# A third buffer for turned q and four moves of work around it in the last pass of a fused SSM and SwiGLU gradient kernel

## The chip, the cores and the metric

The kernel runs on one core of one Trainium2 chip. The metric is the device time of one execution in microseconds (us). A core has five engines with instruction queues of their own: TensorE (PE, matmul; its weight loads are listed as PEld), VectorE (DVE), ScalarE (ACT), GpSimd (POOL) and SyncE (SP), which here only issues DMAs.

## The reference

A forward pass and its gradient with respect to the 14 inputs, for a sequence of L = 2048 rows with D = 576 channels, N = 128 states for each channel and F = 4608 hidden columns, inputs in bfloat16:

```
x  = A_u
xn = layernorm(x)                                 # over D
K  = real(sum_n C * exp(dt * A * l) * (dt * B))   # D x L kernel of the state space model
s  = causal_conv(xn, K) + xn * Dskip
h  = silu(xn @ w1) * (xn @ w3)
g  = silu(h @ w2)
out = x + s * g
grads = vjp(out)(grad_out)                        # for every input
```

## The kernel before, in words

The forward pass and most of the backward pass come first. The change is in the **last pass**, `phase6_inputs`, from about 1326 us to the end. It makes the gradient of x. The 2048 rows are 16 tiles of 128 rows. For each tile, 72 products are added up in PSUM (`px`): 36 blocks of the gate's gradient GG against w1 and 36 blocks of the up gradient GU against w3. A product n is two matmuls of 128x288 (L2036; the first two tiles, and the last one, go by other loops, L2072 and L2053). The tile `acts` on the left is loaded from DRAM by transposing DMAs on SP's queue (`load_acts`, L1833), GG and GU apart, two tiles ahead, into the buffer that this tile leaves: GG of tile i + 2 is asked for in the middle of tile i, GU at its end.

When a tile's products are done, `ln_bwd_tile` takes it back through the layernorm: VectorE adds the rows `gxs` to `px` (gx, L2105), ScalarE and VectorE form two means (L2155, L2158), GpSimd scales them (sc, L2163 and L2164), ScalarE makes `gxs` from them (L2165), GpSimd adds the rows `go` (L2166). The **last sum** of a tile, which makes its rows of out_1, is apart in `ln_finish`: one VectorE instruction (go, L2171), then a store on ScalarE's queue; for tiles 10 to 13 also two turned stores on GpSimd's queue (L2177). It is called after product n = 8 of the next tile. The rows gxs and go are loaded by SP (L2020, L2021) in `begin`.

Two other pieces of work are put between the products.

- **Steps** (`param_step`, `param_half`). The gradients of the model's parameters need, for each of 36 groups of channels (ch) in two halves, 8 small matmuls (et_ps, L1523) of a turned q (`qT`) against `gz`, then two products on VectorE (pr_q, L1528), each followed by a sum into `S_all` (L1531). The loads of a group (`param_loads`) are asked for two groups ahead, qT by SP, gz (L1508) and pz (L1511) by GpSimd; there are two buffers for qT. The tuple `stops` names the products behind which a step stands: (42, 66) in tile 2, (30, 60) in tile 3, (20, 50) in tiles 4, 6 and 9, none in 0, 1 and 15, and (14, 38, 62) in the others.
- **Blocks** (`phase5_blocks`), a generator that `phase5_step` moves on by one `yield` at each step. Each of five blocks of parameter rows loads `X_b` (L1589, GpSimd), takes ST from the finished sums S_all (L1594, L1595) and products of X_b (L1601 to L1603); then, one yield later, TensorE turns ST (four transposes, L1608, the **turn** of a block) and ScalarE copies it back (L1610); then VectorE makes four outputs (L1614 to L1616), which GpSimd stores (L1620), and so on up to L1637. After the last block, TensorE turns one small tile (L1641).

The steps' and the blocks' PSUM tiles come from one pool (`ps_T`) and one tile more (`ps_X`). Every queue runs in the order in which the program issues. `issue_after` binds an instruction's place behind another one in that order.

Of the kernel before, what the change touches and what calls it, by code (L numbers as in the profile page):

```python
# [14 lines left out]
BF16 = mybir.dt.bfloat16  # L15
I32 = mybir.dt.int32
I16 = mybir.dt.int16
P = 128
# [82 lines left out]
class K:  # L101
# [1231 lines left out]
    def params_open(self, S_all, ps):  # L1333
        cfg = self.cfg
        self.sums = ExitStack()
        gkp = self.sums.enter_context(self.pool(name="g_k", bufs=1, side="right"))
        self.qp = self.sums.enter_context(self.pool(name="g_q", bufs=2, side="right"))
        self.zp = self.sums.enter_context(self.pool(name="g_z", bufs=3, side="right"))
        self.prp = self.sums.enter_context(self.pool(name="g_pr", bufs=1, side="right"))
        self.S_all, self.ps_T = S_all, ps  # L1340
        self.gz = []
        for i in range(3):
            z = gkp.tile([P, 2, 2, 2, 8, cfg.LT], BF16, name=f"gz{i}")
            self.nc.vector.memset(z[:], 0.0)
            self.gz.append(z)
        self.half = 0
        self.apart = False
        self.ps_X = None
        self.loaded = {}

    def param_step(self):
        nch = self.cfg.D // 16
        if self.half == 2 * nch:
            return
        ch, dg = divmod(self.half, 2)
        with self.tc.issue_after(self.pe_last.ins):
            self.param_half(ch, dg, *self.loaded[ch])
        if dg == 1 and ch + 2 < nch:
            if self.hold is None:
                self.loaded[ch + 2] = self.param_loads(ch + 2)  # L1360
            else:
                self.hold.append(ch + 2)
        self.half += 1
# [12 lines left out]
    def conv_bwd_quarter(self, g, kp, zp, ps, T0, TQ):  # L1376
# [102 lines left out]
        for j in range(NB - 1, -1, -1):  # L1479
# [18 lines left out]
            nc.scalar.dma_start(out=self.GXN_dram[:, j * KT:(j + 1) * KT, cs], in_=gx[:])  # L1498

    def param_loads(self, ch):  # L1500
        nc, cfg = self.nc, self.cfg
        g, cc = divmod(ch, cfg.D // 64)
        gK = self.gz[ch % 3]
        qT = self.qp.tile([P, 16, cfg.N], BF16, name="qT")
        self.nat_transpose(qT[:], self.Q_dram[ch])
        put, q = (self.gp, nc.gpsimd) if self.apart else (self.sp, nc.sync)
# [8 lines left out]
    def param_half(self, ch, dg, gK, qT, pz):  # L1515
        nc, AV = self.nc, self.cfg.AV
# [8 lines left out]
        for x in range(2):  # L1525
# [4 lines left out]
                                    in1=pz[:, dg * 2 + x][:, :, None, :].to_broadcast([P, 2, 4, 4 * AV]), op=ALU.mult)  # L1530
            nc.vector.tensor_reduce(out=self.S_all[:].rearrange("p r (h c) -> p r h c", h=2)[:, :, :, d0:d0 + 2],  # L1531
                                    in_=pr[:].rearrange("p r k (h j a) -> p (r k) h j a", h=2, j=2), op=ALU.add, axis=AX.X)
# [40 lines left out]
    def phase5_blocks(self):  # L1573
# [6 lines left out]
        for j, c0 in enumerate(range(0, H, 64)):  # L1580
# [22 lines left out]
            tt(out=W[v, 1], in0=Q[v, 0, 1], in1=Q[v, 1, 0], op=ALU.add)  # L1603
            yield 0
            pt = self.ps_T.tile([P, 4, N], FP32, name="et_ps")
            with self.tc.issue_after(self.pe_last.ins):
# [40 lines left out]
    def backward(self, T0, TG, TQ, TC, TX, gctx, mats):  # L1647
# [11 lines left out]
        with ExitStack() as out:  # L1659
            wp = out.enter_context(pool(name="e_w", bufs=2))  # L1660
            self.rowp = rowp = out.enter_context(pool(name="e_w2r", bufs=1))
# [18 lines left out]
            self.hn = {}  # L1680
            self.w2Ts = {}
            self.ggs = {}
            self.tail = None
# [117 lines left out]
            wT[:-3] = sorted(wT[:-3], key=lambda part: part[0])  # L1801
            ffn.close()
            self.phase6_inputs(T2, TX, wT, acts, pool)
            self.sums.close()
# [40 lines left out]
    def phase6_load_w2(self, gi, wp):  # L1845
        nfl = self.FG // P
        w2T = wp.tile([P, nfl, self.cfg.DT, P], BF16, name="w2T")
        for fl in range(nfl):
            with self.tc.issue_after(self.hc_loads[13].ins) if gi == 0 else nullcontext():
                self.nat_transpose(w2T[:, fl], self.w2rows[gi % 2][:, fl])  # L1850
# [156 lines left out]
    def phase6_inputs(self, T2, TX, wT, acts, pool):  # L2007
# [7 lines left out]
        with pool(name="l_sb", bufs=2) as sb, pool(name="l_s1", bufs=1) as s1, \  # L2015
# [16 lines left out]
            def product(i, px, n0, n1, stops):  # L2032
                for n in range(n0, n1):
                    ai, fi, w = (sides if i else steps)[n]
                    for pi_, (po, pw) in enumerate(pieces):
                        self.pe_last = nc.tensor.matmul(px[pi_][:, 0:pw], lhsT=acts[i][:, ai, fi, :], rhs=w[:, po:po + pw],  # L2036
                                                        start=(n == 0), stop=(n == len(steps) - 1))
                    if n == 8 and i > 1:
                        self.ln_finish()
                    if n == cfg.FT - 1 and 1 < i < LT - 2:  # L2040
                        self.load_acts(i + 2, (0,), acts[i])
                    if n in stops:
                        self.param_step()
                        self.phase5_step(self.half // 2)

            n1, n2, n3 = self.ready, self.ready + 14, len(steps)
# [39 lines left out]
            acts.append(self.load_acts(3, (0,), acts[1]))  # L2086
            self.param_flush()
            blocks(1, late, True)
            self.load_acts(3, (1,), acts[1])
            for i in range(LT):  # L2090
                self.at(T2 + TX * i)
                t = self.order[i]
                px, gxs, go_t, o1, _ = opened[i] if i < 2 else begin(i)
                if i == 1:
# [9 lines left out]
                for pi_, (po, pw) in enumerate(pieces):  # L2104
                    nc.vector.tensor_tensor(out=gx[:, po:po + pw].rearrange("p (g d) -> p g d", g=4),  # L2105
                                            in0=px[pi_][:, 0:pw].rearrange("p (g d) -> p g d", g=4),
                                            in1=self.perm(gxs[:])[:, :, pi_, :], op=ALU.add)
                self.ln_bwd_tile(sm, gx, gxs, i, t, go_t, o1)
                if 1 < i < LT - 2:
                    acts.append(self.load_acts(i + 2, (1,), acts[i]))  # L2110
# [169 lines left out]
```

## Time and profile before

| | |
|---|---|
| runs | 1678.49, 1654.67, 1642.81 us; median 1654.67 |
| profiled execution | 1651.06 us, span 1648.9 us |
| TensorE | busy 1575.2 us (96% of the span) |
| VectorE | busy 1385.5 us (84%) |
| ScalarE | busy 838.3 us (51%) |
| GpSimd | busy 517.4 us (31%) |
| granted TensorE clock, mean over the span | 0.989 |
| last pass | about 1326 to 1649 us |

A time is read as follows: a run is one execution, and the profile is of another one of the same program. Busy time of an engine counts its instructions without the waits between them. In the rows of the profile, `[5.79 <-DVE ST L1594]` behind an instruction says that its engine was idle for 5.79 us before it and that VectorE's instruction of line 1594 ended the wait.

### The profile page before, as it was taken

The page shows a single profiled execution, that of the slowest core. Times are in us where ns is not written, and L with a number is a line of the kernel's source. Part 1 is how long each engine was busy: PE and PEld are TensorE (multiplying, and loading weights), DVE is VectorE, ACT ScalarE, POOL GpSimd, SP SyncE. Part 2 cuts the span into 40 slices and gives each one's busy share as a digit, 9 for nine tenths or more (in the row PEclk, how much of TensorE's full clock was granted, in tenths as well). Part 3 has the DMA queues.
Part 4 walks back from the last instruction along what each step waited for, and adds up shares of the span by engine and source line. Part 5 has one row for each costly group of instructions (what it writes and reads, how often), then busy time and mean ns, then how long its engine had stood idle before and what let it go on. Part 6 is the DMA issues. An engine that isn't in the chain of part 4 may idle for free. (4 is left out here: it accounts for less than half of the span.)

```text
span 1648.9 us, 34389 instructions
## 1 busy us (share of the span) xinstructions
PE 1575.2 (96%) x13331; PEld 1150.1 (70%) x13331; DVE 1385.5 (84%) x2145; ACT 838.3 (51%) x1520; POOL 517.4 (31%) x862
## 2 busy tenths in 40 slices
PE   6899999999999998999999999999999999989988
PEld 2554444444457776888888888888888787868866
DVE  8889998799965655998978999699989945788788
ACT  6989998766642115556555565555555301011011
POOL 7746766532242110111111111112212343325241
PEclk9999999999999999999999999999999999999999
DMA  7999999987999996576695756899999999999992
GB/s 239 347 335 360 373 344 376 380 264 249 316 294 218 240 224 207 157 213 194 191 258 161 214 185 184 234 228 253 257 244 258 243 252 232 249 211 214 210 236 64
DMA packets 616156, 408.26 MB, mean 248 GB/s; under 512 B 424698, under 2 KB 558426, under 8 KB 611386
## 3 DMA queue, kind: packets, MB, share of 16 engines
q1 hardware_dynamic: 561232, 277.45, 67.1%
q0 software_dynamic: 36576, 116.69, 21.8%
q10 hardware_dynamic: 18186, 11.95, 2.5%
q8 instruction: 104, 1.70, 0.4%
q14 instruction: 58, 0.48, 0.1%
HBM read 128.52 MB, written 188.76 MB: 192 GB/s over the span
## 5 line engine op out<-in xcount | busy, mean ns | idle before, releaser
L1982 PEld LDWEIGHTS <-xn_bf 128*128 128x128 bf16 x2304 | 224.4, 98 | 34.4 <-issue 8.2
L2036 PEld LDWEIGHTS <-acts 128*128 128x128 bf16 x1974 | 193.2, 99 | 49.3 <-issue 0.2
L1967 POOL DMA_DIRECT2D out_dram<-gw x72 | 47.3, 657 | 532.5 <-ACT gw L1984 313.4
L1528 DVE TENSOR_TENSOR pr_q<-et_ps,pz 128x1024 f32<-128x1024 f32 x144 | 175.9, 1221 | 27.5 <-PE et_ps L1523 20.1
L1123 PEld LDWEIGHTS <-xnT 128*128 128x128 bf16 x1152 | 107.8, 98 | 127.8 <-issue 20.2
L1531 DVE TENSOR_REDUCE S_all<-pr_q 128x32 f32<-128x1024 f32 x144 | 175.2, 1217 | 3.2
L1916 PE MATMUL ph<-w2T,goT 128*128 128x256 bf16 x1440 | 169.7, 273 | 1.4 <-ACT gh L1919 1.4
L1123 PE MATMUL pg<-wmB_w,xnT 128*128 128x512 bf16 x576 | 156.8, 381 | 1.3 <-DVE g_t L1142 1.0
L1957 PE MATMUL pgw<-go_o,h_n 128*128 128x288 bf16 x1152 | 153.9, 288 | 1.0 <-ACT gw L1963 1.0
L1916 PEld LDWEIGHTS <-goT 128*128 128x128 bf16 x1440 | 139.1, 98 | 18.7 <-issue 2.9
L1123 PE MATMUL pu<-wmB_w,xnT 128*128 128x512 bf16 x576 | 149.7, 379 | 0.0
L2036 PE MATMUL px<-wT,acts 128*128 128x288 bf16 x1134 | 147.3, 288 | 0.0
L1982 PE MATMUL pgw<-gu_n,xn_bf 128*128 128x256 bf16 x1152 | 133.0, 272 | 3.6 <-ACT gw L1963 3.1
L1957 PEld LDWEIGHTS <-h_n 128*128 128x128 bf16 x1152 | 112.7, 98 | 29.2 <-issue 2.1
L1982 PE MATMUL pgw<-gg_n,xn_bf 128*128 128x256 bf16 x1152 | 130.3, 273 | 0.4 <-ACT gw L1984 0.4
L1919 ACT CAST gh<-ph 128x512 bf16<-128x512 f32 x144 | 80.5, 589 | 85.1 <-PE ph L1916 78.6
L1138 ACT ACTIVATE s_t<-pg 128x512 bf16<-128x512 f32 x144 | 88.3, 613 | 55.9 <-PE pu L1132 43.9
L2155 ACT ACTIVATE go<-gx 128x576 bf16<-128x576 f32 x15 | 10.2, 683 | 185.1 <-DVE gx L2105 158.0
L813 POOL COPY KT<-k_s 64x128 bf16<-64x128 bf16 x144 | 85.1, 591 | 53.7 <-ACT k_s L810 49.0
L2036 PE MATMUL px<-wA,acts 128*128 128x288 bf16 x728 | 97.3, 290 | 0.0
L1143 ACT CAST u_t<-pu 128x512 bf16<-128x512 f32 x144 | 87.3, 606 | 6.3 <-PE pu L1123 6.2
L1152 POOL DMA_DIRECT2D G_dram<-g_t x72 | 51.5, 716 | 120.0 <-ACT g_t L1140 93.8
(338 smaller groups left out, 3244.5 us busy)
## 6 DMA issues: line engine op xcount, KB each, us to landing
U_dram<-u_t POOLq DMA_DIRECT2D x72, 256.0 KB, 6.1
H_dram<-h_t SPq DMA_DIRECT2D x72, 256.0 KB
G_dram<-g_t POOLq DMA_DIRECT2D x72, 256.0 KB, 5.7
Q_dram<-q_k SPq DMA_DIRECT2D x36, 512.0 KB
GG_dram<-gg_n SPq DMA_DIRECT2D x36, 512.0 KB
GU_dram<-gu_n SPq DMA_DIRECT2D x36, 512.0 KB
gg_n<-G_dram POOLq DMA_DIRECT2D x14, 1024.0 KB, 6.5
E_dram<-E_k SPq DMA_DIRECT2D x54, 256.0 KB
```

The lines of the kernel that those rows point to most:

```text
L813: nc.gpsimd.tensor_copy(out=KT[64 * hf:64 * hf + 64, :, ch // 9, h, d1:d1 + 8], in_=ks[64 * h:64 * h + 64, :, h, hf].rearrange("p d a -> p ...
L1123: ins = nc.tensor.matmul(pt[:], lhsT=xnT[:, c, ts], rhs=wm[w][:, c, :], start=(q == 0 and c == 0), stop=(q == 1 and c == nfull - 1))
L1138: nc.scalar.activation(out=s_t[:, :, q, :], in_=pgv, func=ACT.Silu)
L1143: self.gate_last = nc.scalar.copy(out=u_t[:, :, q, :], in_=puv)
L1152: self.u_stores[step] = nc.gpsimd.dma_start(out=dst[fb * ng:(fb + 1) * ng, :, i0:i0 + NT, :].rearrange("g p t f -> p g (t f)"), in_=src[:] ...
L1528: nc.vector.tensor_tensor(out=pr[:].rearrange("p r k e -> p r (k e)"), in0=T[x][:].rearrange("p z k h j a -> p (z k h j a)")[:, None].to_b ...
L1531: nc.vector.tensor_reduce(out=self.S_all[:].rearrange("p r (h c) -> p r h c", h=2)[:, :, :, d0:d0 + 2], in_=pr[:].rearrange("p r k (h j a) ...
L1916: self.pe_last = nc.tensor.matmul(ph[j][:, k, :].rearrange("p (a f) -> p a f", f=P), lhsT=lw, rhs=rh, start=(n == 0), stop=(n == nfull))
L1919: self.sc(lambda: nc.scalar.copy(out=gh[:, j], in_=ph[j][:]))
L1957: self.pe_last = nc.tensor.matmul(pgw[pi_][:, 0:pw], lhsT=hn[:, tt, fl * P:(fl + 1) * P], rhs=go_o[:, tt, po:po + pw], start=(tt == 0), st ...
L1982: self.pe_last = nc.tensor.matmul(pw_[:, 0:FG], lhsT=self.xn_bf[:, tt, c * P:(c + 1) * P], rhs=nat[:, tt, :], start=(tt == 0), stop=(tt == ...
L2036: self.pe_last = nc.tensor.matmul(px[pi_][:, 0:pw], lhsT=acts[i][:, ai, fi, :], rhs=w[:, po:po + pw], start=(n == 0), stop=(n == len(steps ...
```

## The change

Four edits, all in the last pass:

1. **Third buffer for the turned q.** The pool `e_w`, which before had two buffers of w2T, now has one double tile of w2T and is free in the last pass. One of every three qT is placed there, and each qT is asked for three groups ahead instead of two (`param_q`, `qTs`, `third`). gz and pz stay two groups ahead.
2. **Last sum later.** `ln_finish` is called at the next tile's first step, if that is at product 20 or before, and bound behind that step's last sum in S_all; else after product 8, as before.
3. **Turn later.** A second `yield 0` ahead of a block's turn, in all blocks but the last.
4. **Rows ahead of GU.** `begin(i + 1)` is called at the end of tile i ahead of GU's load, instead of at the start of tile i + 1.

```diff
 def param_step(self):
...
         if dg == 1 and ch + 2 < nch:
             if self.hold is None:
                 self.loaded[ch + 2] = self.param_loads(ch + 2)
+                if self.third and ch + 3 < nch:
+                    self.third[1] = self.third[1] or ch
+                    self.qTs[ch + 3] = self.param_q(ch + 3, None if (ch - self.third[1]) % 3 else self.third[0])
...
+    def param_q(self, ch, third=None):
+        if third is None:
+            qT = self.qp.tile([P, 16, self.cfg.N], BF16, name="qT")
+        else:
+            qT = third.tile([P, 16, self.cfg.N], BF16, name="qT", tag="w2T")
+        self.nat_transpose(qT[:], self.Q_dram[ch])
+        return qT
+
     def param_loads(self, ch):
...
-        qT = self.qp.tile([P, 16, cfg.N], BF16, name="qT")
-        self.nat_transpose(qT[:], self.Q_dram[ch])
+        qT = self.qTs.pop(ch, None)
+        if qT is None:
+            qT = self.param_q(ch)
...
 def param_half(self, ch, dg, gK, qT, pz):
...
-            nc.vector.tensor_reduce(out=self.S_all[:].rearrange("p r (h c) -> p r h c", h=2)[:, :, :, d0:d0 + 2],
+            self.pr_last = nc.vector.tensor_reduce(out=self.S_all[:].rearrange("p r (h c) -> p r h c", h=2)[:, :, :, d0:d0 + 2],
...
 def phase5_blocks
...
             yield 0
+            if c0 + R < H:
+                yield 0
             pt = self.ps_T.tile([P, 4, N], FP32, name="et_ps")
...
 # the w2 loads of an earlier phase
-            wp = out.enter_context(pool(name="e_w", bufs=2))
+            wp = out.enter_context(pool(name="e_w", bufs=1))
...
-        w2T = wp.tile([P, nfl, self.cfg.DT, P], BF16, name="w2T")
+        if self.w2TT is None:
+            self.w2TT = wp.tile([P, 2, nfl, self.cfg.DT, P], BF16, name="w2T")
+        w2T = self.w2TT[:, gi % 2]
...
 def product(i, px, n0, n1, stops):
...
-                    if n == 8 and i > 1:
-                        self.ln_finish()
                     if n == cfg.FT - 1 and 1 < i < LT - 2:
                         self.load_acts(i + 2, (0,), acts[i])
                     if n in stops:
                         self.param_step()
                         self.phase5_step(self.half // 2)
+                    if i > 1 and n == (stops[0] if stops and stops[0] <= 20 else 8):
+                        with self.tc.issue_after(self.pr_last.ins) if n != 8 else nullcontext():
+                            self.ln_finish()
...
             self.param_flush()
+            self.third = [self.wp, 0]
             blocks(1, late, True)
...
-                px, gxs, go_t, o1, _ = opened[i] if i < 2 else begin(i)
+                px, gxs, go_t, o1, _ = opened[i]
...
                 self.ln_bwd_tile(sm, gx, gxs, i, t, go_t, o1)
+                if i:
+                    opened.append(begin(i + 1))
                 if 1 < i < LT - 2:
                     acts.append(self.load_acts(i + 2, (1,), acts[i]))
```

Up to the last pass the instructions of both programs stand in the same order on every engine. The places where they differ most are shown next, before and after; the changed program's line numbers are up to 24 higher.

SP's queue in the last pass, where the third buffer comes in (gxs and go are the rows of a tile; the number in a name is that of the buffer). Before:

```order
L2020 DMA gxs_19217<-GXN_dram 128x576
L2021 DMA go_19218<-odd_grad_out 128x576
L1833 DMA_TRANSPOSE acts<-GG_dram 128x36x128
L1833 DMA_TRANSPOSE qT<-Q_dram 128x16x128
L1833 DMA_TRANSPOSE acts<-GU_dram 128x36x128
L2020 DMA gxs_19450<-GXN_dram 128x576
L2021 DMA go_19451<-odd_grad_out 128x576
```

With the change, the same place:

```order
L2040 DMA gxs_19193<-GXN_dram 128x576
L2041 DMA go_19194<-odd_grad_out 128x576
L1851 DMA_TRANSPOSE acts<-GG_dram 128x36x128
L1851 DMA_TRANSPOSE qT<-Q_dram 128x16x128 x2
L2040 DMA gxs_19406<-GXN_dram 128x576
L2041 DMA go_19407<-odd_grad_out 128x576
L1851 DMA_TRANSPOSE acts<-GU_dram 128x36x128
```

One load of qT more stands here once, and from here on each qT is one group ahead of its place before; the rows gxs and go stand ahead of GU.

VectorE around tile 5's last sum and the sums ST of block 2 (the second row pair `mgx` is the mean of the tile; `go` is the last sum). Before:

```order
L2158 ISA pr_q,mgx<-gx_19877,xn_bf 128x576
L2158 ISA mgx 128x1
L2171 SCALAR_TENSOR_TENSOR go_19874<-gx_19877,rstd,gxs_19873 128x576
L1528 TENSOR_TENSOR pr_q<-et_ps,pz 128x1024
L1531 TENSOR_REDUCE S_all<-pr_q 128x16x2
L1528 TENSOR_TENSOR pr_q<-et_ps,pz 128x1024
L1531 TENSOR_REDUCE S_all<-pr_q 128x16x2
L1594 TENSOR_TENSOR ST<-S_all 128x256
```

With the change:

```order
L2182 ISA pr_q,mgx<-gx_19862,xn_bf 128x576
L2182 ISA mgx 128x1
L1542 TENSOR_TENSOR pr_q<-et_ps,pz 128x1024
L1545 TENSOR_REDUCE S_all<-pr_q 128x16x2
L1542 TENSOR_TENSOR pr_q<-et_ps,pz 128x1024
L1545 TENSOR_REDUCE S_all<-pr_q 128x16x2
L2195 SCALAR_TENSOR_TENSOR go_19858<-gx_19862,rstd,gxs_19857 128x576
L1608 TENSOR_TENSOR ST<-S_all 128x256
```

The last sum has moved behind the first step's two products and sums.

TensorE at the turn of block 2. Before, it stands behind the step at product 50 of tile 6:

```order
L1523 LDWEIGHTS qT
L1523 MATMUL et_ps<-gz_14621,qT 128x2x2x32
L1608 MATMUL et_ps<-ident_f,ST 128x128 x4
L2036 LDWEIGHTS acts
L2036 MATMUL px_20092<-wT_15_18326,acts 128x288
```

With the change, it stands behind the step at product 14 of tile 7:

```order
L1537 LDWEIGHTS qT
L1537 MATMUL et_ps<-gz_14611,qT 128x2x2x32
L1624 MATMUL et_ps<-ident_f,ST 128x128 x4
L2056 LDWEIGHTS acts
L2056 MATMUL px_20290<-wT_15_18307,acts 128x288
```

Between the two places lie 36 products of TensorE. In the same way block 1's turn has moved from the loops of the first two tiles to the second step of tile 2, and block 3's from product 38 to product 62 of tile 12; those of blocks 0 and 4 stand where they stood.

More of the change, by code (lines that the diff above doesn't have):

```diff
@@ L1349, in params_open @@
         self.loaded = {}
+        self.qTs = {}
+        self.third = None
     def param_step(self):
@@ L1846, in phase6_load_w2 @@
         nfl = self.FG // P
-        w2T = wp.tile([P, nfl, self.cfg.DT, P], BF16, name="w2T")
+        if self.w2TT is None:
+            self.w2TT = wp.tile([P, 2, nfl, self.cfg.DT, P], BF16, name="w2T")
+        w2T = self.w2TT[:, gi % 2]
         for fl in range(nfl):
-            with self.tc.issue_after(self.hc_loads[13].ins) if gi == 0 else nullcontext():
+            with self.tc.issue_after(self.hc_loads[13].ins) if gi < 2 else nullcontext():
                 self.nat_transpose(w2T[:, fl], self.w2rows[gi % 2][:, fl])
```

2 lines of the change are left out of this document (added).

## The prediction

> **What bounds the kernel now.** First the page's head, then the busy time by stretch of the last pass.
>
> ```profile
> span 1648.9 us, 34389 instructions
> ...
> PE 1575.2 (96%) x13331; PEld 1150.1 (70%) x13331; DVE 1385.5 (84%) x2145; ACT 838.3 (51%) x1520; POOL 517.4 (31%) x862
> ```
> ```profile
> 1451.00:1468.00 17.00, 11.26 (x78) 8.62 (x79) 13.37 (x19) 2.48 (x5) 1.89 (x5) 0.80 0.66 150
> 1468.00:1568.00 100.00, 100.00 (x883) 81.09 (x882) 82.78 (x96) 7.75 (x15) 37.33 (x67) 1.00 1.16 214
> 1568.00:1584.00 16.00, 10.70 (x71) 7.92 (x69) 13.00 (x17) 1.71 (x3) 3.13 (x5) 0.79 1.13 263
> ```
> After the stretch and its length come the busy times of PE, PEld, DVE, ACT and POOL, then the granted clock. TensorE is the bound: in 100 us it is busy for 100. It stops twice, and both times its clock falls, to 0.80 and 0.79. The build order of the two programs is the same on every engine until about 1326 us, so only this pass can change. Next, what TensorE waited for there:
>
> ```profile
> PE et_ps L1608 <- DVE ST L1594: 5.8, 1, 5.8
> ...
> PE et_ps L1523 <- DMA qT<-Q_dram: 5.6, 2, 5.3
> ```
> One wait is for the turn of a block (L1608), whose sums VectorE had not made; the other for a turned q that had not landed.
>
> **What the two stops cost.** Starts and times on TensorE (a step is the 8 small matmuls L1523 and the two product-and-sum pairs of VectorE behind them, L1528 and L1531; between steps stand the tiles' main products, two matmuls each):
>
> ```profile
> 1450.34 0.61 PE L1523 MATMUL et_ps<-gz,qT 128*128 128x128 bf16 x8
> 1456.74 1.08 PE L1608 MATMUL et_ps<-ident_f,ST 128*128 128x128 f32 x4 [5.79 <-DVE ST L1594]
> ...
> 1467.91 0.61 PE L1523 MATMUL et_ps<-gz,qT 128*128 128x128 bf16 x8
> ...
> 1515.14 0.61 PE L1523 MATMUL et_ps<-gz,qT 128*128 128x128 bf16 x8
> ...
> 1524.40 0.61 PE L1523 MATMUL et_ps<-gz,qT 128*128 128x128 bf16 x8
> ...
> 1562.43 0.61 PE L1523 MATMUL et_ps<-gz,qT 128*128 128x128 bf16 x8
> ...
> 1574.22 1.04 PE L1523 MATMUL et_ps<-gz,qT 128*128 128x128 bf16 x8 [5.30 <-DMA qT<-Q_dram]
> ...
> 1583.84 0.61 PE L1523 MATMUL et_ps<-gz,qT 128*128 128x128 bf16 x8
> ...
> 1590.16 0.61 PE L1523 MATMUL et_ps<-gz,qT 128*128 128x128 bf16 x8
> ```
> ```profile
> 1633.06 0.44 PE et_ps L1608 x4
> ```
> From one step to the next takes 1524.40 - 1515.14 = 9.26 us where 36 products stand between them, 1590.16 - 1583.84 = 6.32 where 24 do, and a turn 0.44. The first stop: behind the step at 1450.34 stand a turn and 36 products, so the next was due 9.70 later, at 1460.04, and came at 1467.91: 7.87. The second: from the step at 1562.43 over that at 1574.22 to that at 1583.84 are 21.41 where 2 x 6.32 and a turn, 13.08, were due: 8.33. Together **16.2 us**, of which 5.79 + 5.30 is idling and 5.1 (2.1 and 3.0) the slower clock behind it.
>
> [...]
>
> **The turn one step later.** VectorE's rows before the first stop:
>
> ```profile
> 1378.83 1.29 DVE L1614 TENSOR_TENSOR pr_q<-ST,X_b 128x512 f32<-128x512 f32 x2
> ...
> 1380.50 0.42 DVE L1616 SCALAR_TENSOR_TENSOR WO_b<-pr_q 128x256 bf16<-128x256 f32 x1
> ...
> 1399.89 0.82 DVE L2171 SCALAR_TENSOR_TENSOR go<-gx,rstd,gxs 128x576 bf16<-128x576 f32 x1 [2.32 <-POOL gxs L2166]
> ...
> 1414.76 1.22 DVE L1528 TENSOR_TENSOR pr_q<-et_ps,pz 128x1024 f32<-128x1024 f32 x1
> ...
> 1419.92 1.23 DVE L1528 TENSOR_TENSOR pr_q<-et_ps,pz 128x1024 f32<-128x1024 f32 x1
> ...
> 1450.35 0.82 DVE L2171 SCALAR_TENSOR_TENSOR go<-gx,rstd,gxs 128x576 bf16<-128x576 f32 x1 [2.65 <-POOL gxs L2166]
> ```
> ```profile
> DVE go L2171 <- POOL gxs L2166: 27.0, 11, 3.9
> ```
> A step's two products and two sums take 1419.92 - 1414.76 = 5.16 us. Block 2's turn ran at 1456.74, as soon as its sums ST were there; it is now asked for one step later, at 1460.04 + 0.45 = 1460.5. So the later turn alone takes the first stop away, unless VectorE becomes 3.8 us later still. Block 1's turn moves from the start of the pass, where VectorE idles, into tile 2, and its L1614 to L1616 (1378.83 to 1380.92: 2.1 us) behind later sums, onto the loaded engine: even with that, and with no wait gone, the turn could run at 1458.8.
>
> **The last sum behind the next step's sums.** VectorE's last sums (L2171) wait for GpSimd's add, 27.0 us in 11 waits of the last pass, 2.45 each. Four of them, the first of 2.32 and the last of 2.65, stand ahead of block 2's ST: an estimated 9.8. The first stays (tile 2 has no early step, so tile 1's last sum is issued after the ninth product, as before); the three others get 5.16 us of other work ahead of them. The turn could then run by 1456.74 - 9.8 + 2.5 + 2.1 = 1451.5, 9 us ahead of its new place. Worth on its own: nothing, since TensorE does not wait then; it is the margin. Queued behind the sum are its store on ScalarE's queue and the next rows on SP.
>
> **The third buffer.** SP's queue before the second stop:
>
> ```profile
> 1543.97 2.80 SPq L1833 DMA_TRANSPOSE qT<-Q_dram  x1
> 1546.87 11.11 SPq L1833 DMA_TRANSPOSE acts<-GU_dram  x1
> ...
> 1559.17 9.10 SPq L1833 DMA_TRANSPOSE acts<-GG_dram  x1
> 1568.37 2.35 SPq L1833 DMA_TRANSPOSE qT<-Q_dram  x1
> ```
> ```profile
> L1833 SPq DMA_TRANSPOSE acts<-GG_dram x16: 1245/5522/10057, 1328.2 to 1596.0; - x16
> ```
> The late load was behind a GU and a GG that held SP for 11.11 and 9.10 us, against a median of 5.52 for GG. With a third buffer each load is queued one channel (two steps) earlier: the place of the load at 1543.97 is now the stalled channel's. Less the 7.9 us won before it, that is 1536, and it is wanted at 1562.43 + 6.32 - 7.9 = 1560.9: a margin of 25 us, from which two transposes as slow as these take 9.2 more than the median. The second stop goes: between nothing and 8.3, I take 8.3.
>
> Its price: one load more stands ahead of tile 4's GU, which was issued at 1393.85 and is wanted at 1409.11:
>
> ```profile
> 1393.85 6.32 SPq L1833 DMA_TRANSPOSE acts<-GU_dram  x1
> ...
> 1400.26 0.53 SPq L2020 DMA_DIRECT2D gxs<-GXN_dram  x1
> ```
> ```profile
> 1409.11 2.86 PE L2036 MATMUL px<-wA,acts 128*128 128x288 bf16 x22
> ```
> With 2.8 us for the q and 1.0 for the rows now ahead, it is issued by 1404: 5 us before its use. Nothing, at most 3 if it lands slowly; I take nothing.
>
> **Rows ahead of GU.** SP now waits for the last sum and its store before GU, not after. GU of tile i+2 has the whole tile i+1 and half of i+2 as cover, some 28 us (a tile is 18.98: three stretches of 6.32); its price is nothing while a sum comes within that. The rows come earlier, which is again margin.
>
> **What comes late next.** The end of the pass:
>
> ```profile
> 1556.53 1.23 DVE L1528 TENSOR_TENSOR pr_q<-et_ps,pz 128x1024 f32<-128x1024 f32 x1 [0.61 <-PE et_ps L1523]
> ...
> 1584.26 1.23 DVE L1528 TENSOR_TENSOR pr_q<-et_ps,pz 128x1024 f32<-128x1024 f32 x1 [2.69 <-PE et_ps L1523]
> ...
> 1642.12 0.15 DVE L1637 TENSOR_TENSOR sm_b<-sm_b 64x1 f32<-64x1 f32 x1
> ```
> ```profile
> 1642.41 0.27 PE L1641 MATMUL et_ps<-ident_f,sm_b 128*5 128x128 f32 x1
> ```
> The last turn (L1641) follows VectorE's last small sum at 1642.27 by 0.14 us: there is no margin at the end. At 1556.53 and at 1584.26 VectorE had caught up with TensorE, the second time thanks to the stop. Without it, VectorE has between these two steps 3 x 5.16 us, a tile's own work, and the first part of block 3 (L1594 to L1603, estimated like the 2.1 of L1614 to L1616 above), while TensorE takes 18.98. The tile's own work by the groups of the last pass, beside the last sum's 0.82:
>
> ```profile
> L2105 DVE TENSOR_TENSOR gx<-px,gxs 128x288 f32<-128x288 f32 x30 | 13.0, 449 | 28.3 <-PE px L2072 15.1 <-DMA gxs<-GXN_dram 12.1 <-PE px L2036 1.0
> L2158 DVE CUSTOM_DVE_ANT_0 pr_q<-gx,xn_bf 128x576 f32<-128x576 f32 x15 | 11.4, 758 | 0.5
> ```
>
> That is 2 x 0.45 + 0.82 + 0.76 = 2.5, in all 20.1: VectorE is 1.1 us late from there on, and every wait behind it adds to that. POOL's order makes one likelier: block 3's stores and reloads, one step later, now stand ahead of tile 13's scale (L2163), and with it ahead of the add for which tile 13's last sum waits. The longest such wait among the 11 above is 3.9. So the end loses between 0 and 1.1 + 3.9 = 5 us; I take **1.5**, near the low end, since the add is due only behind a step's sums (5.16).
>
> **The sum.** 7.9 + 8.3 - 1.5 = **14.7 us** against the profiled execution's 1651.06 (span 1648.9): 1636.4. The median of the runs shown is 1654.67, 3.6 above the profiled one, with runs from 1642.81 to 1678.49; the same ratio, 0.991, makes 1639.9 of it. I say 1638.
>
> **Rivals.** One step on TensorE and its first product on VectorE, for the slower one:
>
> ```profile
> 1442.54 0.61 PE L1523 MATMUL et_ps<-gz,qT 128*128 128x128 bf16 x8
> ```
> ```profile
> 1451.08 1.22 DVE L1528 TENSOR_TENSOR pr_q<-et_ps,pz 128x1024 f32<-128x1024 f32 x1
> ```
>
> - *One stop's worth is kept.* SP stays behind: the slow transposes fall in with the turned stores of out_1, which still run. Or VectorE bounds the last tiles, with waits for GpSimd that don't go. For it: 82.78 us of VectorE's 100 are busy above. Against: the margins of 25 and 9 us. It gives 1651.1 - 8 = 1643. [...]
> - *It does not do what it says*: the third buffer's load is held by something that I misread, or the turn's wait moves along with it. 1651, or 1654 against the median.
> - *Slower: the step after a turn waits for VectorE.* A turn takes one of three PSUM buffers, so the following step needs the product of the step just before, not of two steps before. The step at 1442.54 was multiplied only at 1451.08, 8.5 us late. If VectorE is late by more than 6.32 + 0.44 - 1.25 = 5.5 us at a turn, TensorE stops there; at the 12 us that the buffers allow, for 6.5 us and 3 more of slow clock, at three turns 28.5. That is 1651.1 - 14.7 + 28.5 = 1665. Against it: only blocks 1 to 3 turn later, and with the waits for GpSimd gone the sum of the end finds VectorE late by 1.1 us there, not 5.5.
> - *No wait at the end*: 16.2, so 1635.
>
> **How the numbers follow.** Forecast 0.60, no wait at the end 0.08, one stop kept 0.20, no effect 0.08, slower by the turns 0.04. The cases from 1635 to 1654 hold 0.96; the runs before scatter from 12 below to 24 above their median, and a median of a few runs by perhaps 12, so the range is 1623 to 1662. 2% of the time is 33 us, about what a measurement of this kernel can tell from no change. No case reaches that, only scatter: faster by over 2% 0.06, within 2% 0.91, slower 0.03.
>
> **What would show it.** Right: TensorE's waits in the last pass without L1608 for ST and with no q wait over 1 us; granted clock 1.00 from 1373 to the last turn; VectorE's wait for GpSimd's add at 27.0 us falling to under 10; a wait of 1 to 2 us ahead of the last turn. Wrong: a new wait of TensorE for pr_q behind a turn, for GU at a tile's middle, or for q again; VectorE's last sum of tile 13 held by GpSimd for more than 4 us.

## The result and the profile after

The changed kernel takes 1640.15 us (median of 18 runs, 1630.33 to 1658.06), the kernel before 1650.93 us (18 runs that go with them, 1640.47 to 1678.49). The ratio is 0.9939, with a 95% interval of 0.9914 to 0.9964: about 10 us less. Comparisons of times leave out executions of over 1.5% above the fastest of their kernel, and three profiles further down are of such executions: without the late sum (1667.92 us), without the third buffer (1666.10), rows by ScalarE and the end (1660.29). The profiled execution took 1640.91 us against 1651.06. Its page's head, then the last pass by the same stretches (us, busy PE, PEld, DVE, ACT, POOL, granted clock, then the busy share of the DMA engines and GB/s):

```profile
span 1639.1 us, 34391 instructions
...
PE 1568.0 (96%) x13331; PEld 1145.2 (70%) x13331; DVE 1384.4 (84%) x2145; ACT 837.0 (51%) x1520; POOL 516.6 (32%) x862
```
```profile
1451.00:1468.00 17.00, 17.00 (x154) 13.91 (x152) 12.91 (x15) 2.48 (x5) 3.46 (x6) 1.00 1.15 243
1468.00:1568.00 100.00, 96.56 (x848) 77.94 (x847) 83.84 (x101) 8.62 (x16) 38.24 (x68) 1.00 1.21 219
1568.00:1584.00 16.00, 16.00 (x142) 13.05 (x140) 15.20 (x18) 2.48 (x5) 3.42 (x6) 1.00 1.16 242
```

Both stops are gone: TensorE is busy for all of the 17 and the 16 us in which it was busy for 11.26 and 10.70, at a clock of 1.00. But between them it is now idle for 3.4 us of 100, where before it was busy throughout. What TensorE and VectorE waited for (us in total, times, longest):

```profile
DVE go L2195 <- POOL gxs L2190: 15.4, 7, 2.9
...
DVE gx L2127 <- DMA gxs<-GXN_dram: 14.0, 4, 5.3
...
PE px L2056 <- DMA acts<-GG_dram: 2.5, 2, 1.6
...
PE et_ps L1657 <- DVE sm_b L1653: 2.2, 1, 2.2
...
PE px L2056 <- DMA acts<-GU_dram: 1.9, 1, 1.9
```

TensorE's rows at the places of the two stops, at the two new waits between them, and at the end; then two slow loads in SP's queue ahead of the new waits:

```profile
1450.83 0.61 PE L1537 MATMUL et_ps<-gz,qT 128*128 128x128 bf16 x8
...
1460.10 0.61 PE L1537 MATMUL et_ps<-gz,qT 128*128 128x128 bf16 x8
1460.55 0.61 PE L1624 MATMUL et_ps<-ident_f,ST 128*128 128x128 f32 x4
...
1517.04 0.61 PE L1537 MATMUL et_ps<-gz,qT 128*128 128x128 bf16 x8
...
1524.67 0.91 PE L2056 MATMUL px<-wA,acts 128*128 128x288 bf16 x6 [1.88 <-DMA acts<-GU_dram]
1525.42 0.61 PE L1537 MATMUL et_ps<-gz,qT 128*128 128x128 bf16 x8
...
1531.74 0.61 PE L1537 MATMUL et_ps<-gz,qT 128*128 128x128 bf16 x8
...
1536.12 3.85 PE L2056 MATMUL px<-wA,acts 128*128 128x288 bf16 x30 [1.56 <-DMA acts<-GG_dram]
1539.80 0.61 PE L1537 MATMUL et_ps<-gz,qT 128*128 128x128 bf16 x8
...
1558.78 0.61 PE L1537 MATMUL et_ps<-gz,qT 128*128 128x128 bf16 x8
...
1578.20 0.61 PE L1537 MATMUL et_ps<-gz,qT 128*128 128x128 bf16 x8
...
1609.84 0.61 PE L1537 MATMUL et_ps<-gz,qT 128*128 128x128 bf16 x8
...
1632.59 0.27 PE L1657 MATMUL et_ps<-ident_f,sm_b 128*5 128x128 f32 x1 [2.23 <-DVE sm_b L1653]
```
```profile
1463.93 11.24 SPq L1851 DMA_TRANSPOSE acts<-GU_dram  x1
...
1512.78 8.74 SPq L1851 DMA_TRANSPOSE acts<-GU_dram  x1
```

The account, from the first step of tile 0 (1333.21 before, 1333.13 now) to the last turn (1642.41 and 1632.59): 309.2 us before, 299.5 now, 9.7 less.

| place | before | now | gained |
|---|---|---|---|
| first stop (step at 1450.34 / 1450.83 and the two behind it) | 23.90 | 16.04 | 7.9 |
| second stop (three stretches from 1562.43 / 1558.78) | 27.73 | 19.42 | 8.3 |
| GU late in tile 10 (1517.04 to 1525.42, due 6.33) | | 8.38 | -2.1 |
| GG late for tile 11 (1531.74 to 1539.80, due 6.32) | | 8.06 | -1.7 |
| from the last step to the last turn (1621.80 / 1609.84) | 20.61 | 22.75 | -2.1 |

These make 10.2 before rounding; 0.6 is lost ahead of the step at 1450, where GG came late for tile 2 and block 1's turn now stands.

This account compares one execution with one. A second profile of the kernel before (in the next section) has a pass of only 299.9 us, 0.4 more than the changed kernel's: it has no second stop, and its first stop, 6.8 us, is about what the changed kernel loses at GU, at GG, at the end and ahead of the step at 1450. So the length of the pass in one profile does not show the gain; the ratio of the runs does.

### The profile page after: what moved, and what is told of

It is laid out like the page before. It is cut to its first block, busy times and chain, and to the rows that moved or that the text cites. A ratio compares the mean times of both kernels' runs of the same rounds, so it can differ in the third digit from the quotient of the medians.

```text
span 1639.1 us, 34391 instructions
## 1 busy us (share of the span) xinstructions
PE 1568.0 (96%) x13331; PEld 1145.2 (70%) x13331; DVE 1384.4 (84%) x2145; ACT 837.0 (51%) x1520; POOL 516.6 (32%) x862
## 5 line engine op out<-in xcount | busy, mean ns | idle before, releaser
L2179 ACT ACTIVATE go<-gx 128x576 bf16<-128x576 f32 x15 | 10.2, 683 | 195.3 <-DVE gx L2127 189.0
```

## The experiments

The four edits (the third buffer and three moves) were taken out one by one, and three of them were put into the kernel before alone. Each kernel has a profile, from which come two measures beside the time: what TensorE waited for in the last pass, and the length of the pass. Profiled executions of one kernel differ, also ahead of the last pass (tile 0's first step stands at 1333.21 us in one profile of the kernel before, at 1334.33 in the other), and the intervals of the times are some 0.4% wide to either side, each against runs of the kernel before on the same chip. In three groups of runs that kernel's medians were 1653.08, 1648.92 and 1647.03, so the medians of rows of different groups can't be compared. A ratio seldom tells two of these kernels apart either, while the waits name causes. Line numbers differ by a few between the kernels.

| kernel | median, us | ratio to before, 95% interval | tile 2's first step to last turn, us | TensorE's wait for ST of block 2 / q / GG and GU / VectorE's product, us |
|---|---|---|---|---|
| before | 1650.93 | | 269.1 | 5.8 / 5.6 / 0 / 0 |
| before, a second profile | | | 259.8 | 5.2 / 0 / 0.3 / 0 |
| changed | 1640.15 | 0.9939 [0.9914, 0.9964] | 259.2 | 0 / 0 / 4.4 / 0 |
| without the later turn | 1641.44 | 0.9959 [0.9914, 1.0004] | 262.6 | 0 / 0 / 6.3 / 0 |
| without the late sum | 1646.98 | 0.9985 [0.9943, 1.0026] | 270.5 | 0 / 0 / 4.6 / 6.4 |
| without the third buffer | 1646.47 | 0.9988 [0.9948, 1.0029] | 282.5 | 0 / 12.6 / 12.1 / 0 |
| rows behind GU again | 1638.94 | 0.9949 [0.9905, 0.9992] | 262.8 | 0 / 0 / 0.5 / 5.2 |
| later turn alone | 1649.06 | 1.0015 [0.9974, 1.0057] | 265.9 | 0 / 0 / 1.8 / 6.1 |
| late sum alone | 1641.89 | 0.9962 [0.9919, 1.0005] | 252.7 | 0 / 0 / 1.5 / 0 |
| third buffer alone | 1647.93 | 0.9990 [0.9943, 1.0038] | 262.6 | 5.8 / 0.2 / 0 / 0.4 |
| end: late sum of tile 14 | 1641.33 | 0.9964 [0.9923, 1.0004] | 257.8 | 0 / 0.5 / 4.0 / 0 |
| rows by ScalarE | 1640.84 | 0.9950 [0.9918, 0.9981] | 254.7 | 0 / 0.5 / 0.4 / 0 |
| rows by ScalarE, no third buffer | 1639.52 | 0.9972 [0.9940, 1.0005] | 269.7 | 0 / 14.3 / 1.8 / 0 |
| rows by ScalarE and the end | 1636.89 | 0.9957 [0.9926, 0.9988] | 261.0 | 0 / 0.4 / 6.2 / 0 |

### The first stop: the later turn or the late sum

Without the later turn:

```diff
             yield 0
-            if c0 + R < H:
-                yield 0
```

> The changed kernel without the later turn (no second yield ahead of a block's turn); third buffer, late last sum and early rows stay. The pass is measured in the profile from the first step of tile 0 to the last turn of one small tile: 309.2 us before, 299.5 after. Theory A, that the late last sum alone frees the first stop too: in the profile of the change block 2's ST was ready at 1449.9, ahead of the old place of the turn at 1451.3; so no wait of TensorE for ST over 1 us, the pass 299.5 (298 to 301), the time as the change (ratio to before 0.994). Theory B, that only the later turn removes this stop: a wait for ST of 4 to 6 us, its slow clock behind it, the pass 307, ratio 0.998.

TensorE's rows of block 2's and block 3's turns:

```profile
1449.38 0.60 PE L1622 MATMUL et_ps<-ident_f,ST 128*128 128x128 f32 x4
...
1566.69 1.06 PE L1622 MATMUL et_ps<-ident_f,ST 128*128 128x128 f32 x4 [2.09 <-DVE ST L1608]
```

Block 2's turn is back at its old place and does not wait: theory A. The pass is 303.5, not 299.5, for two reasons that A had left out: block 3's turn waits for 2.09 at its old place, and GU was late three times, for 5.2 us (GG once, for 1.1).

Without the late sum:

```diff
+                    if n == 8 and i > 1:
+                        self.ln_finish()
                     if n == cfg.FT - 1 and 1 < i < LT - 2:
...
-                    if i > 1 and n == (stops[0] if stops and stops[0] <= 20 else 8):
-                        with self.tc.issue_after(self.pr_last.ins) if n != 8 else nullcontext():
-                            self.ln_finish()
```

> The changed kernel with the last sum after product 8 of the next tile, as before; third buffer, later turn and early rows stay. Theory A, that the later turn alone frees the first stop: ST by about 1458, the turn asked for at 1460.5, no wait for ST over 1 us; VectorE's waits for GpSimd's add back at 20 to 27 us; the pass 299 to 302, ratio to before 0.994 to 0.996. Theory B, that the margin of the late sum is needed: a wait for ST or, behind a turn, for a product of VectorE, 2 to 6 us, pass 303 to 307, ratio 0.997.

VectorE's waits for GpSimd, TensorE's for VectorE, and TensorE's rows around block 2's turn:

```profile
DVE go L2194 <- POOL gxs L2189: 31.1, 12, 5.3
...
PE et_ps L1537 <- DVE pr_q L1542: 7.0, 4, 3.7
```
```profile
1476.08 0.61 PE L1624 MATMUL et_ps<-ident_f,ST 128*128 128x128 f32 x4
...
1482.40 0.39 PE L1537 MATMUL et_ps<-gz,qT 128*128 128x128 bf16 x4
1484.30 0.38 PE L1537 MATMUL et_ps<-gz,qT 128*128 128x128 bf16 x4 [1.52 <-DVE pr_q L1542]
```

There is no wait for ST, so the later turn, too, frees the turn. But the step behind it now breaks in two: its first four matmuls run, and the second four wait for VectorE to free a PSUM buffer. That is theory B, but this wait costs only 1.7 us (8.01 to the next step, due 6.33). Of the four waits of 7.0 us in all, one of 0.64 falls ahead of the last pass, one of 1.12 in the next tile and the longest, 3.72, at the last step. The whole pass is 310.0, above B's 303 to 307; in it GG was late for 4.61 us, which the late sum does not explain.

Each edit alone on the kernel before:

> The kernel before with the later turn alone. Theory A, that the later turn frees the first stop but, without the late last sum, hands VectorE's delay to the step behind a turn: no wait of TensorE for ST; waits for a product of VectorE (pr_q) of 3 to 7 us in all behind the turns (7.0 in 4 where only the late sum was taken out of the change); q late once or more, 3 to 8; pass (first step of tile 0 to the last small turn, 309.2 before, 299.5 changed) 304 to 310, ratio to before 0.997 to 1.000. Theory B, each edit worth its own stop: no pr_q waits over 1 us, the pass 301 to 302 with q late as before, ratio 0.995.

> The kernel before with the late last sum alone. Theory A, that this edit by itself frees the first stop (the change without the later turn had no wait at block 2's turn): no wait for ST of block 2, less than 2.5 at block 3; q late by 0 to 8 us; from tile 2 to the last turn 259 to 264 (269.1 before), ratio to before 0.995 to 0.998. Theory B, that it frees it only along with earlier rows and loads on SP: the wait for ST stays at 3 to 6 us and the stretch at 265 to 269, ratio 0.999.

The later turn alone, TensorE's wait for VectorE's product and VectorE's for GpSimd, and the longest of each; then, of the late sum alone, VectorE's last sum and block 2's ST, and its turn:

```profile
DVE go L2191 <- POOL gxs L2186: 34.7, 12, 8.9
...
PE et_ps L1537 <- DVE pr_q L1542: 6.1, 5, 2.2
```
```profile
1435.64 0.82 DVE L2191 SCALAR_TENSOR_TENSOR go<-gx,rstd,gxs 128x576 bf16<-128x576 f32 x1 [8.93 <-POOL gxs L2186]
...
1440.22 0.38 PE L1537 MATMUL et_ps<-gz,qT 128*128 128x128 bf16 x4 [2.20 <-DVE pr_q L1542]
```
```profile
1445.03 0.81 DVE L2190 SCALAR_TENSOR_TENSOR go<-gx,rstd,gxs 128x576 bf16<-128x576 f32 x1
1445.76 0.42 DVE L1608 TENSOR_TENSOR ST<-S_all 128x256 f32<-128x256 f32 x1
1446.09 0.42 DVE L1609 TENSOR_TENSOR ST<-S_all 128x256 f32<-128x256 f32 x1
```
```profile
1447.87 0.61 PE L1622 MATMUL et_ps<-ident_f,ST 128*128 128x128 f32 x4
```

The later turn alone shows no gain (1.0015): five waits for VectorE and 2.6 us ahead of the last turn take the place of the stop. Only one of them, 1.33 us, stands behind block 2's turn. The two largest, 1.71 and 2.20, stand at tile 5's third step and cost 5.9 us with the slow clock (the 18 matmuls behind the second took 3.48 us, 18 behind a step without a wait 2.37): there tile 4's last sum holds the ready products of a step up while it waits 8.93 us for GpSimd, whose scaling for it (1432.81) stands behind the loads of the next block's X_b and of gz and pz. The later turn has moved those of X_b there, from 1397 to 1414 us. The late sum alone has ST ready at 1446.51, 1.36 us ahead of the old place of the turn, and its profile has the shortest stretch of all, 252.7. So theory A holds in its main point for both; not in its numbers, for q was late in neither, the pass with the later turn alone is 311.4 (304 to 310 expected, mostly behind the turns), and 252.7 is below 259 to 264. That the late sum alone is the better of the two is shown by the waits; the times point the same way, 0.9962 [0.9919, 1.0005] against 1.0015 [0.9974, 1.0057], though the intervals overlap. No comparison shows that the other three edits add to it: the change as a whole has 0.9939 [0.9914, 0.9964].

### The second stop: the third buffer

```diff
-            self.third = [self.wp, 0]
```

> The changed kernel without the third buffer: each turned q is loaded one channel later, as before the change; the other three edits stay. Theory A, that the second stop comes of the late place of a q in SP's queue: TensorE waits again for q, once or more, 3 to 8 us with the slow clock behind it, and the pass is 303 to 308 instead of 299.5; ratio to before about 0.997. Theory B, that the second stop was an accident of two slow transposes in the profiled execution, and a q is otherwise in time: no wait for q over 1 us, the pass 299 or less, ratio 0.993 or less, since no load more stands ahead of GU and GG and their waits (1.9 and 1.6 us in the change) go.

> The kernel before with the third buffer alone. Theory A: no wait of TensorE for q over 1 us; the wait for ST of block 2 stays at 4 to 7 us with its slow clock; waits for GU or GG of 0 to 4 us; pass 301 to 306, ratio to before 0.995 to 0.997. Theory B, that the first stop, too, came of late loads on SP (rows or gz), which the third buffer changes: the wait for ST under 3 us, pass 299 to 300.

> The kernel before once more, for a second profile. Theory A, that both stops belong to the order of the program: TensorE waits for ST of block 2 for 5 to 7 us and for q for 3 to 8 us, from tile 2 to the last turn 267 to 271 (269.1 in the first). Theory B, that the wait for q hangs on slow transposes that fall elsewhere in every execution: the wait for ST as before, the wait for q under 1 us or at another step, the stretch 259 to 264.

TensorE's wait for q without the third buffer, and three loads that held SP's queue ahead of it; then the third buffer alone and the second profile of the kernel before, both with the first stop and without the second:

```profile
PE et_ps L1537 <- DMA qT<-Q_dram: 12.6, 4, 7.2
```
```profile
1482.31 15.51 SPq L1851 DMA_TRANSPOSE acts<-GU_dram  x1
...
1508.85 13.23 SPq L1851 DMA_TRANSPOSE acts<-GU_dram  x1
1522.17 12.57 SPq L1851 DMA_TRANSPOSE qT<-Q_dram  x1
```
```profile
1454.66 1.09 PE L1622 MATMUL et_ps<-ident_f,ST 128*128 128x128 f32 x4 [5.80 <-DVE ST L1608]
```
```profile
1457.24 1.09 PE L1608 MATMUL et_ps<-ident_f,ST 128*128 128x128 f32 x4 [5.20 <-DVE ST L1594]
```

The first stop is there in every profile without the late sum and the later turn (5.8, 5.2, 5.8). The second is not: of six profiles with two buffers, three wait for q (5.6, 12.6 and 14.3 us) and three do not (second profile of before, later turn alone, late sum alone); of eight with three buffers none waits for more than 0.5. So the third buffer keeps q in time, but against something that an execution has or has not: transposes that hold SP for 8 to 15.5 us instead of a median of 5.2 to 6.0. All profiles but one (rows behind GU) have one to five such among 26 or 27 loads of GG and GU. Without the third buffer there were five, GU too was late, once for 11.06, and the pass was 322.9, far above theory A's 303 to 308. Theory B of the second profile holds for q. A gain in time from the third buffer is not shown: alone it has 0.9990 [0.9943, 1.0038], and the interval of the change without it, 0.9948 to 1.0029, overlaps that of the change.

These long holds are not spread evenly. Over the 14 profiles, of 62 loads of GG and GU that had one of the turned stores of out_1 (GpSimd's queue) in flight in their first 4.4 us, 22 held SP for more than 8 us; of the other 305, 15 did. That fits the prediction's rival, in which slow transposes fall in with these stores. That the stores are the cause was not tried, and 15 came without them, the one of 15.51 among these.

### The rows and SP's queue

Rows behind GU again, and rows by ScalarE's queue:

```diff
-                px, gxs, go_t, o1, _ = opened[i]
+                px, gxs, go_t, o1, _ = opened[i] if i < 2 else begin(i)
...
-                if i:
-                    opened.append(begin(i + 1))
```

> The changed kernel with the rows gxs and go asked for behind GU at the next tile's start, as before; the other three edits stay. Theory A, that the rows ahead of GU hold it and the GG behind it back: TensorE's waits for GU and GG (1.9 and 1.6 us near 1524 to 1536, and 0.9 at 1362) shrink to under 1 in all, and the pass falls by 1 to 3 to 297 to 298. Theory B, that the place of the rows does nothing for TensorE, and single slow transposes make these waits: waits for GU or GG of 0 to 5 us at other places, the pass 298 to 302. VectorE's wait for the rows (14.0 us in 4) grows in either.

```diff
                 if i > 1:
-                    self.sp(lambda: rows(i, gxs, go_o1, nc.sync))
+                    rows(i, gxs, go_o1, nc.scalar)
```

> The changed kernel with the rows gxs and go of tiles 2 to 15 loaded by ScalarE's queue, behind the store of the last sum that frees their buffers, instead of by SP ahead of GU. Theory A, that rows and acts press on one another in SP's queue (rows ahead: 4.3 us of waits of TensorE for GU and GG, and 14.0 us of VectorE for the rows; rows behind: 0.5 and 24.8): off SP, both waits fall, VectorE's for the rows under 5 us, TensorE's for acts under 2, and the pass to 296 to 298, ratio to before 0.992. Theory B, that the waits for GU and GG come of single slow transposes and not of the order: TensorE's waits for acts stay at 2 to 5 us wherever these fall, the pass at 298 to 302.

> The kernel with the rows on ScalarE's queue, without the third buffer. Theory A, that SP's queue is what makes q late, and that with the rows off it a q is in time without a third buffer too: no wait for q over 1 us, from tile 2 to the last turn 254 to 256. Theory B, that two buffers ask for q too late, whatever stands in SP's queue: waits for q of 3 to 8 us, the stretch 258 to 263, ratio to before 0.996.

The rows behind GU, VectorE's wait for them, and block 3's turn; last, with the rows by ScalarE and without the third buffer, TensorE's wait for q:

```profile
DVE gx L2127 <- DMA gxs<-GXN_dram: 24.8, 7, 6.5
```
```profile
1584.44 0.73 PE L1624 MATMUL et_ps<-ident_f,ST 128*128 128x128 f32 x4 [4.64 <-DVE pr_q L1542]
```
```profile
PE et_ps L1537 <- DMA qT<-Q_dram: 14.3, 3, 12.7
```

With the rows behind, GG and GU are in time (0.5 us of waits), but VectorE waits for rows for 24.8 us instead of 14.0, and TensorE for VectorE at a turn, 4.64. No worth of the edit is shown: 0.9949 [0.9905, 0.9992] without it. This is also the one profile without a slow transpose, so that GG and GU came in time may be due to that and not to the order. Off SP, TensorE waited for GU for 0.4 us and VectorE for no rows (stretch 254.7). But in the next kernel of this kind (below) GG and GU were late again for 6.2, so the relief does not hold in every execution. And it does not replace the third buffer: theory B there, with 14.3 us of waits for q, more than its 3 to 8.

### The end

```diff
-            tt(out=self.gl[v, j:j + 1], in0=acc[v, 0:1], in1=acc[v, 2:3], op=ALU.subtract)
+            self.gl_last = tt(out=self.gl[v, j:j + 1], in0=acc[v, 0:1], in1=acc[v, 2:3], op=ALU.subtract)
...
-                    if m == 16:
-                        self.ln_finish()
                     if m in (68, 84, 100, 140):
                         self.phase5_step(self.half // 2)
+                    if m == 104:
+                        with self.tc.issue_after(self.gl_last.ins): self.ln_finish()
```

> The changed kernel with the last sum of tile 14 bound behind the last small sums of block 4 (L1653), instead of after the 17th product of the last tile; its store on ScalarE moves behind ScalarE's copy of block 4's turn. Theory A, that the wait of 2.2 us ahead of the last small turn comes of this sum's wait of 2.65 us for GpSimd and of the store that holds ScalarE's copy: L1653 ends 2.5 to 3 earlier, no wait ahead of the last turn, the time from the last step of tile 14 to that turn 20.5 instead of 22.75; at the end up to 0.7 is given back since the moved sum stands ahead of the last tile's own sums; 1.5 to 2.2 us less in all, ratio to before about 0.993. Theory B, that VectorE's own amount of work sets this end: the wait stays at 1.5 or more.

The end of the changed kernel, in order of time, then TensorE's last turn with the sum moved:

```profile
1623.97 1.27 POOL L2190 TENSOR_TENSOR gxs<-gxs,go 128x576 f32<-128x576 f32 x1 [0.98 <-ACT gxs L2189]
1625.28 0.82 DVE L2195 SCALAR_TENSOR_TENSOR go<-gx,rstd,gxs 128x576 bf16<-128x576 f32 x1 [2.65 <-POOL gxs L2190]
...
1626.82 0.83 ACT L1626 ACTIVATE ST<-et_ps,sm_b 64x256 f32<-64x256 f32 x2 [2.93 <-DVE gx L2155]
1627.32 1.28 DVE L1630 TENSOR_TENSOR pr_q<-ST,X_b 64x512 f32<-64x512 f32 x2 [0.68 <-ACT ST L1626]
```
```profile
1643.74 0.27 PE L1657 MATMUL et_ps<-ident_f,sm_b 128*5 128x128 f32 x1
```

Tile 14's last sum waits for GpSimd, and ScalarE's copy of the turned ST stands behind that sum's store; the small sums for the last turn stand behind both. With the sum moved there is no wait ahead of the turn, and it comes 20.71 us behind the last step instead of 22.75: theory A. Behind the turn 1.5 us are given back (8.06 to the span's end instead of 6.51), more than the 0.7 allowed for, so the whole is about 0.5 us.

The other profiles point to the edit that makes this loss. With tile 14's last sum in its old place, it is 20.5 to 21.0 us from the last step to the last turn in the five profiles without the later turn, the late sum alone among them. In those with it, it is 22.1 to 28.5, except in the two that stopped for q late in the pass (20.4 and 21.5), where VectorE had time to catch up: its last product of a step started 5.25 and 6.31 us behind TensorE's last step, against 7.57 in the changed kernel. So the later turn comes with the loss at the end, while the late sum frees the first stop without it.

> The changed kernel with the rows on ScalarE's queue and tile 14's last sum behind block 4's last small sums. From the first step of tile 2 to the last small turn the profiles had 269.1 us before, 259.2 with the change, 257.8 with the late sum of tile 14, 254.7 with the rows on ScalarE's queue. Theory A, that the two are apart: 254.7 less the 1.6 of waiting ahead of the last turn, 253; no wait of TensorE over 1 us in that stretch; ratio to before 0.990 to 0.992. Theory B, that what is left are single slow transposes that fall where they like: 256 to 260, ratio 0.994.

With both, the end is again without a wait (20.36), but GG was late twice, once for 3.08, and GU once: 261.0, just above theory B's 256 to 260. 1636.89 is the lowest median, yet its ratio, 0.9957 [0.9926, 0.9988], is no better than that of the change. No version was shown to beat it.

## Why the prediction was right, and where its steps were not

- **The sum.** 14.7 us were forecast against the profiled execution, 9.7 came in its pass (span 9.8), and 0.6% in the ratio where 0.9% stood. The sign and the place are right, and the time lies in the range, which was wide enough to hold no change too. Two things were luck. The forecast of 1638 is only 2 us from 1640.15, but the median before came out 3.7 lower with 18 runs (1650.93 for 1654.67). And the 9.7 us hang on the execution that was profiled; against the second profile of before, the pass is 0.4 us shorter. With the second stop at its average of the two profiles, the account's terms make about 5 us, an estimate (7.9 + 4 - 2.1 - 1.7 - 2.1 - 0.6); the interval of the ratio stands for 6 to 14. What fills the gap is open.
- **The first stop, 7.9.** It came to 7.9. But the cause was given to the wrong edit. "The later turn alone takes the first stop away" is true of the wait for ST and not shown for the time (1.0015). Alone, it hands part of the delay on. 1.5 to 1.7 us go to the step behind the turn, which is the mechanism of the rival "the step after a turn waits for VectorE", whose condition, VectorE late by more than 5.5 us at a turn, the two kernels with the later turn and without the late sum met. In one of them 5.9 us more are lost where the last sum, still early, waits for a GpSimd that stands behind loads moved there by the later turn. The prediction had seen this effect of GpSimd's order, but only for block 3. The late sum, priced at "nothing, the margin", is what removes the delay: alone, it frees the old place by 1.36 us. Whether the later turn adds anything beside it is not shown: without it block 3's turn waited for 2.09 us in one profile and not in another, and with it the end is longer.
- **The second stop, 8.3.** It came to 8.3 against that profile. What failed is that the stop was taken as a feature of the program: half of the profiles with two buffers have no wait for q. Against a typical execution the term is smaller; from two profiles of before, one of 8.3 and one of nothing, an estimate is 4.
- **GU and GG.** "I take nothing" for tile 4 held there. The waits came in tiles 10 and 11, 3.8 us. Ahead of them GU held SP for 11.24 and 8.74 us; the rows that now stand ahead of the second took 1.1 (1511.67 to 1512.78). This term was missing; a margin had been worked out for q alone, though GG and GU share its queue.
- **The end, 1.5.** Measured 2.1, and by the mechanism named: VectorE finishes later. Its last product of a step, in the kernel before and in the changed one:

```profile
1627.23 1.22 DVE L1528 TENSOR_TENSOR pr_q<-et_ps,pz 128x1024 f32<-128x1024 f32 x1
```
```profile
1617.41 1.22 DVE L1542 TENSOR_TENSOR pr_q<-et_ps,pz 128x1024 f32<-128x1024 f32 x1
```

  It starts 5.43 us behind TensorE's last step before (at 1621.80) and 7.57 now (at 1609.84): 2.14 more, as much as the loss. The hold by GpSimd that was feared for tile 13's last sum was small (1.28 us). Tile 14's last sum waits for 2.65, but it waited for 2.66 before, so this is not what is new; moving that sum takes an old wait out of the chain and so pays for the delay.
- **Rows ahead of GU, nothing.** As far as the ratios tell, right (0.9949 without this edit, 0.9939 with it). That two effects cancel here, TensorE's waits for acts and VectorE's for the rows, is argued from one profile of each.
- **The signs.** No wait for ST, none for q and a clock of 1.00 from 1373 to the last turn came as forecast. VectorE's wait for GpSimd's add fell from 27.0 to 15.4, not under 10, and the wait ahead of the last turn was 2.2, not 1 to 2. One sign of being wrong did appear, a wait for GU at a tile's middle (1.88). And 0.6% could be told from no change, where the prediction allowed for 2%.
- **The clock behind a stop.** Beyond its idling, the first stop cost 2.1, 1.6 and 2.9 us in three profiles (the kernel before 7.87 - 5.79, its second profile 6.84 - 5.20, the third buffer alone 8.70 - 5.80), and the granted clock from 1451 to 1468 was 0.80, 0.90 and 0.80. So the 2.1 taken from one profile gives this cost to about a microsecond, no closer.

## What to carry to other kernels

Here a wait was better cured where its delay came from (a sum that waits for another engine, put behind work that is ready; no wait was left at block 2's turn) than where it showed: the consumer moved later passed part of the delay on to the next buffer (1.5 to 1.7 us), and moved other work with it. A stall behind a transfer in one profile may be an accident of that execution (5.6 us of waits for q in one profile of the kernel before, none in the other): take a second profile of the same kernel before it is put into a sum at full price. The third buffer kept q in time (no wait over 0.5 us in eight profiles), but each load that a deeper buffer moves ahead stands in front of others in the same queue, whose margins have to be worked out too.

## What was not expected of the hardware

Equal transposes of 128x36x128 held SP from 4.4 to 15.5 us, with a median of 5.2 to 6.0 in each profile. The long holds fell at other places in the two executions of even the same program (in the kernel before at 1515, 1547 and 1559 us, then once, at 1521), though often beside the turned stores (22 of 37). What the profile shows is how long the load held the queue; when its data landed is not in it.

The clock did not follow from the length of the wait alone. In one execution (without the later turn) it fell after a wait of 2.09 us, to 0.50 in the next 3 us, and stayed at 1.00 after one of 3.29:

```profile
1567.00:1570.00 3.00, 3.00 (x15) 2.06 (x14) 2.84 (x6) 0.84 (x2) 0.00 (x0) 0.50 1.17 294
```
```profile
1544.00:1547.00 3.00, 2.84 (x28) 2.38 (x29) 1.64 (x2) 0.00 (x0) 1.08 (x2) 1.00 1.47 198
```
```profile
1544.16 0.91 PE L2054 MATMUL px<-wA,acts 128*128 128x288 bf16 x6 [3.29 <-DMA acts<-GU_dram]
```

The first row is behind block 3's turn, the second behind a late GU, whose wait stands in the last row.
